# A new table of instruction orders for a fused cluster-attention, Fourier and feed-forward kernel on one Trainium2 core

## The chip, the cores and the metric

The kernel is one program on one core of one Trainium2 chip. Its metric is the device time of an execution in microseconds (us). The core has five instruction streams that run beside each other and meet at semaphores: TensorE (PE in the profile; PEld is its loading of weights into the array), VectorE (DVE), ScalarE (ACT), GpSimd (POOL) and SyncE (SP), which here does nothing but issue DMAs. Each stream runs its instructions strictly in the order in which they stand in the program.

## What is computed

Four sequences of 768 tokens go through clustered attention with 8 heads of 64, then through a two-dimensional Fourier transform with a residual, a normalization and a feed-forward layer of 512 to 2048 to 512:

```python
mask = q_assign[:, :, :, None] == k_assign[:, :, None, :]
scores = scale * np.matmul(q, k.transpose(0, 1, 3, 2))
scores = np.where(mask, scores, -1000000000.0)
attn = np.exp(scores - np.max(scores, axis=-1, keepdims=True))
attn = attn / (np.sum(attn, axis=-1, keepdims=True) + 1e-09)
x = np.matmul(attn, v)
...
mixed = np.real(np.fft.fft(np.fft.fft(x, axis=1), axis=2))
u = x + mixed
un = (u - mu) / np.sqrt(var + 1e-06)
out = u + np.maximum(un @ w_ch1, 0.0) @ w_ch2
```

The cluster of a query or key is the centroid of largest cosine; the mask keeps pairs of the same cluster.

## The kernel before

All matrix products are made of float16 pieces (a high and a low half), so that each product of the reference is three matmuls.

**Attention.** The 32 heads are taken as 16 pairs, and each pair as six blocks of 128 queries. For one block `Attention.scores` writes the scores of both heads into the two buffers `ps_big` of PSUM. In pairs 0 to 7 these are matmuls of line 538, which use 64 rows of the array each, one head in the upper and one in the lower half, and four mask matmuls of 32 rows (line 543); in pairs 8 to 15 they are the matmuls of line 530, over the whole height. For each head DVE then scales and finds the row's extreme (line 557), ACT takes the exponential (line 560) and rounds it (line 568, tile `ph` or `p`), POOL makes the low half (line 569), and SP issues a DMA that transposes the 128x1536 result into `pts` or `u` (line 571). Two blocks later `Attention.attend` multiplies by v (lines 589 to 591, 18 matmuls per head, tile `ps_o`), and `finish` divides (lines 601 to 605).

**Weights.** Meanwhile `Weights` loads both matrices in 32 pieces (line 715, 512 KB each), finds their scales (line 725) and splits them (lines 754, 758, 764 to 770).

**Layer.** When the four pairs of a sequence are done, its layer runs beside the attention of the next sequence: folding (line 899; line 904 is its transposing DMA), tables from HBM (lines 972 to 982), the transform (lines 991 to 1069), the normalization (line 1120 and about), the up product (line 1286, 160 groups of 12 matmuls into PSUM banks `ps_fa`, `ps_fb`, `ps_fc`, drained by lines 1291 to 1295) and the down product (line 1314, drained by line 1318). For the last sequence, lines 1177 and 1228 to 1253 do two thirds of the up product with fewer multiplications.

**The order.** The code records all instructions in one pass. Then `Order.apply` (in the class `Order`) takes a permutation for each engine out of the table `ORDERS`, a compressed list of 16-bit numbers, and chains the engine's instructions in it:

```python
by = np.cumsum(np.frombuffer(zlib.decompress(base64.b85decode(ORDERS[e])), np.int16))
xs = [xs[n] for n in np.argsort(np.arange(len(xs)) + by)]
for a, b in zip(xs, xs[1:]):
    self.tc.add_manual_dep(b, a.name, ...)
```

Tiles, buffers, banks and dependencies were fixed by the recording; the table alone says which instruction of an engine stands behind which.

Of the kernel before, what the change touches and what calls it, by code (L numbers as in the profile page):

```python
# [26 lines left out]
P = 128  # L27
B, H, S, D = 4, 8, 768, 64
# [4 lines left out]
SH = S // 2  # L33
# [34 lines left out]
class Counted:  # L68
# [5 lines left out]
    def tile(self, shape, dt, name, bufs=None, **kw):  # L74
# [6 lines left out]
        "c-m!E*>2Q85G;?!dyx?3P=fM+1W16y|9=Hf@CG6h2qXyNNV4o{dz<R&@d9Ek+vAz(?&|95SpcZ8v&47ed(5w`ZLG6n#INSv8j#W8qxts{_td;w`%"  # L81
        "b%4+1EJ3OY3cdOMZ8DXBF;ql<~oqc8Nod-PSF9bWq~m@;btdD?3`;+Lj(>T<I;-|COEMggz1$*3fIqr@w0?Vd#iw%ekN2eMalfrkqb&aeR$p-Ev&"
        "fYiA=y$?_9<)r<prY^~BtWa4uNd~TJ+NFFoRT=DS;H}tc#8KYjnF*jVBaL1H0&f3a6w;!DE^_^%@GuD`6&uvLYoX<+vXR`L7puVv~+Kk2f9izlA<"
        "E=eWCV{wN&d!fBmhjFV!N<LM)-j8cNxUm;im#;H7IqI=Y;5@T7`~qH-h8KL;`Z)s#~rO^2ZcD6mOIuK-aBD!Z6uptM4x0)?-d2@a&F^y$~t{vl|I"
        "QHitW)Rs#sE_5x=9d(_-bbjjHVkdJBA&qWLr8jEKPTWjO9$N*i*IoO1EDrS-OO5|!^uo-vd4T#CtHsVQ??+ZCLUvTEGZIFXYqep@QTV>`l)`pLU$"
        "Za#MPy7k<GpCP}wg%*H`d`0Y9os>DAs#mh=)JQ3=55OzGV7xc-)|LF4qLj7u(%Aw1hjKg@uU@bPaZpPsEA>YDk8RKRg%D?4m8?3c8M2Q^6`3D85A"
        "r{#HPo1>eedDk2IiU)Y0XI98Eg5Ddqs??sM|65y|FXKKi>CZL<j{Wv9>CB!+Y?#v|w|%=2CZDU8z^-Y$fi7{43?{?Br72r7Dy#>{^z*fN_br)`{c"
        "RQ=Ju!`eJ1daV>piss(s1{nmJ8VO^Cxvg*4kd>-RlQDfG5u-Nk!YVth`#hMfat!=ii*o^3oxc&^UZRoKXqHZ3cm4~N1Ie<7b0(bRSw`D10A+<*pb"
        "2$Y9<3!92=%dQ9uj47Ou+Zz=nmwm=sn>GfKSR7f9)^2s3H3koJ4@xODrZV9&)0TNUhi|X*`Jr*FQNH!uAlHf2W0dIae2?2aCF3z7P!#rjpqCm|7t"
        "_$jKqsqa4Ke3e7EAM(c67{A5DS6Yo}9rEaZKuw=?t`V5Bny"  # L90
    ),
    "Pool": (
        "c-l==?M~EC5S`wBvb(S=f)b2|m>7+T{`N_HMc=@LKfVKM3{goy(I|$9EbLdeJ)SwYD{j*6?R4hM%$YMadtev1WhWTg6!+{iYV>W%(+PI%3|H8;eS"
        "3*xG^lKh+h$gy#R91X%lMS=3cOOg#2I62+_jH*B71y0N1>>KehUQ4t%31sutd*VB#d41K1ZpTq5WZoROc}^80DVE*p~i|nb|dRog9D1eiAF|{BwI"
        "|hj9CpF=bc9jCS{S+)NcERuM6=-^|e9ksZ)u%5E3R<v44KO&Oapresvsbunfa3HvxAM+2Lv183nEE4-u3!3uS@`VINkS?Zbd`+*s9Wp^Gj@v<jAg"
        "N=B<qEBx7^s1QMYskAS&U(SK+ZxVo%4##R=e6~TQg;5K%lnXBoMVmg1yP5r_7JB;TC%@deNDx5kBs_%MXyZr$kkJ#E)sU{_iLWV7!Ym1xJ>NKafB"
        "E44URU(mYHg8G#_Uv)$GljJMYkQx8g4<r&RVSK4Fu-ZhepE;wJVx!3-niY1oIWBr0Z&F>#(7tS08E?5(gf+oXmjoR!D#(JNP7eMS#y+wbz{s>ZeF"
        "GhLU(XA!d(WVn#p=BT8CsPt`4vnKimvp63^+TLiQuJyod1$jRb>I_jaZmXr<1tP13Dwq*DB}T<Jd-fHpxlQq%_$4vj>QnWYRn<W#j_R0!S(A?IR{"
        "32=16HuZ-OlxVL3Rsr;y#%+%{_gi3gX3yw21q>;Dr0+()YocJwOoph|gPg%BKk)Gp0|hK4*8%Ey(N@;yiP89d~n=x^Vtn>y36g))~aZKpPbqb=|+"
        "iQ{t_whSXjo5u?j4a@T$!leSvid~-@EqLFrUodcDTv4S9dx&0dF+>cHAR*b3@9cx&M#n36yQ3@%)rGMQqa*X?Yw_-Nd?{$sz^ab&Ib+hT=-zoX;-"  # L100
        "*-0dcVWJ-Dd%&F)fdmYjq`kQ-#k~zm`l#r>vpB|c)yS~Tk6F%?V5~VzFdrY)L*G**&q"
    ),
# [26 lines left out]
    "PE": (
        "c-rk8ZEO@(@b#`9&|E(#HB{^e!nL+VT50Qns1+$fsfvkT2#tshiJ&B!C`Ljg8bw>RQDcmvrl@HQ+8X&Gi7_C=)L67?m5PRt5UU{=`~dujBH_8aw`"  # L130
        "<?-?d+Smn`_d9N$#%qc6Mgoyf>fwu3=%qDQUikg+GL>_nf5h3hVu#6oC*5zAXA>GUr=_9xg=SJg<?h3K;J&?t548zy?5uLi;n<dVj{i8bDB+iojV"
        "fvjVR_Yw#+_;+fqtjfOYNuqaTz*NSYhE^&oPzwH_cOw9_!Yzq;*mTP!@Xk0(WG_RE!UcJEeA!B?7)9T)%kzu2CJ!ZVjHLkR^*e_$E#k`wI6KxtPE"
        "@j+J*J^mhjn_^KXMl-gtJM3seEaXHrR}*|pDOGX(ZNy~OvzlqHq<P#wHS*v^ZWp~{-U`mOuD{HBSVjM{chvc$;9zyL<EW}-}f5$9ZbCIG`!o*d0I"
# [728 lines left out]
class Fourier:  # L862
# [7 lines left out]
    EF, AM, EM = 20480, 36992, (42208, 43936)  # L870
# [455 lines left out]
class Overlap:  # L1326
# [4 lines left out]
    T0, LAG = 5, 2  # L1331
# [257 lines left out]
```

## Time and profile before

| what | value |
|---|---|
| time, median of 3 executions | 954.57 us |
| lowest and highest | 952.27 and 954.65 us |
| span of the profiled execution, first to last instruction | 949.3 us |
| PE busy | 863.9 us (91%) |
| DVE, ACT, POOL busy | 678.2, 601.6, 608.3 us |
| mean granted TensorE clock | 0.976 of full speed |

Of the profiled execution only the span is listed, not a time of its own; the timed executions lie 3.0 to 5.4 us above that span. An engine's busy time is the union of its instructions, so what is missing to the span is idle time. An idle stretch is put down to what ended it ("DVE ... <- PE ...": DVE waited for PE); "issue" means that the profile shows no wait. DMA share is the mean busy share of the 16 DMA engines and can go over 1 where packets overlap.

### The profile page before, as it was taken

The page shows a single profiled execution, that of the slowest core. Times are in us where ns is not written, and L with a number is a line of the kernel's source. Part 1 is how long each engine was busy: PE and PEld are TensorE (multiplying, and loading weights), DVE is VectorE, ACT ScalarE, POOL GpSimd, SP SyncE. Part 2 cuts the span into 40 slices and gives each one's busy share as a digit, 9 for nine tenths or more (in the row PEclk, how much of TensorE's full clock was granted, in tenths as well). Part 3 has the DMA queues.
Part 4 walks back from the last instruction along what each step waited for, and adds up shares of the span by engine and source line. Part 5 has one row for each costly group of instructions (what it writes and reads, how often), then busy time and mean ns, then how long its engine had stood idle before and what let it go on. Part 6 is the DMA issues. An engine that isn't in the chain of part 4 may idle for free.

```text
span 949.3 us, 23660 instructions
## 1 busy us (share of the span) xinstructions
PE 863.9 (91%) x9241; PEld 581.0 (61%) x9241; DVE 678.2 (71%) x1531; ACT 601.6 (63%) x944; POOL 608.3 (64%) x752
## 2 busy tenths in 40 slices
PE   4777776677999999998999999999999999999998
PEld 1334443345756748666758667667668586676674
DVE  7989888877756667677757567678773446889643
ACT  6989988776666747647757747657676563353320
POOL 3778786755876876746767768748677764342421
PEclk9999897889999999999999999999999999999999
DMA  9999999988588888999899889998887764201020
GB/s 360 242 217 192 233 262 222 224 169 159 103 169 144 146 178 164 184 177 173 157 171 184 174 155 187 197 173 187 151 147 153 132 118 101 60 1 41 19 78 23
DMA packets 405151, 150.20 MB, mean 158 GB/s; under 512 B 383024, under 2 KB 391728, under 8 KB 405040
## 3 DMA queue, kind: packets, MB, share of 16 engines
q1 hardware_dynamic: 404896, 148.67, 78.1%
q8 instruction: 72, 1.18, 0.5%
q14 instruction: 39, 0.32, 0.1%
q10 hardware_dynamic: 144, 0.03, 0.0%
HBM read 41.99 MB, written 6.29 MB: 51 GB/s over the span
## 4 chain that ended last, share of the span: by engine, by line
PE 56%; DMA 7%; DVE 5%; POOL 4%; ACT 4%; issue 2%; SPq 1%; ACTq 0%; POOLq 0%; DVEq 0%
PE ps_fb L1314 8%; PE ps_fc L1314 7%; DMA pts<-ph 7%; PE ps_fa L1286 6%; PE ps_fa L1314 5%; PE ps_fb L1286 5%; PE ps_fc L1286 5%; PE ps_big L530 5%; PE ps_big L1228 3%; POOL ph L569 2%; PE ps_o L589 2%; PE ps_o L590 2%; PE ps_o L591 2%; PE ps_big L538 1%; ACT ph L568 1%
## 5 line engine op out<-in xcount | busy, mean ns | idle before, releaser
L569 POOL TENSOR_TENSOR ph<-p,ph 128x768 f16<-128x768 f32 x144 | 238.4, 1656 | 112.8 <-ACT ph L568 96.8
L557 DVE TENSOR_SCALAR_CACHE_REDUCE ps_big<-ps_big,sce 128x768 f32<-128x768 f32 x144 | 145.4, 1020 | 60.5 <-PE ps_big L530 34.7
L1314 PEld LDWEIGHTS <-arena 128*128 128x128 f16 x1152 | 109.9, 98 | 121.4 <-issue 1.6
L560 ACT ACTIVATE p<-ps_big,rmx 128x768 f32<-128x768 f32 x144 | 128.7, 897 | 60.3 <-DVE ps_big L557 43.0
L568 ACT CAST ph<-p 128x768 f16<-128x768 f32 x144 | 119.6, 830 | 70.0 <-DMA pts<-ph 67.7
L1295 POOL TENSOR_TENSOR arena<-arena 128x256 f16<-128x256 f32 x160 | 110.8, 697 | 52.2 <-ACT arena L1294 51.6
L1286 PEld LDWEIGHTS <-w1h 128*128 128x128 f16 x1280 | 124.9, 98 | 17.9 <-issue 1.5
L589 PE MATMUL ps_o<-v,pts 128*128 128x66 f16 x1062 | 111.1, 194 | 3.9 <-DMA pts<-ph 2.1
L590 PE MATMUL ps_o<-v,pts 128*128 128x64 f16 x1062 | 110.3, 195 | 0.0
L591 PE MATMUL ps_o<-v,pts 128*128 128x66 f16 x1062 | 110.0, 193 | 0.0
L589 PEld LDWEIGHTS <-pts 128*128 128x128 f16 x1062 | 98.4, 97 | 13.7 <-issue 5.9
L590 PEld LDWEIGHTS <-pts 128*128 128x128 f16 x1062 | 98.4, 97 | 7.4 <-issue 2.6
L1314 PE MATMUL ps_fb<-w2h,arena 128*128 128x512 f16 x320 | 100.9, 379 | 0.0
L591 PEld LDWEIGHTS <-pts 128*128 128x128 f16 x1062 | 98.6, 99 | 0.4
L538 PE MATMUL ps_big<-u 64*128 64x384 f16 x576 | 71.7, 356 | 26.2 <-ACT p L560 13.0
L1286 PE MATMUL ps_fa<-arena,w1h 128*128 128x256 f16 x464 | 85.5, 273 | 0.0
L1314 PE MATMUL ps_fc<-w2h,arena 128*128 128x512 f16 x256 | 81.0, 379 | 0.3 <-ACT arena L1294 0.3
L1286 PE MATMUL ps_fb<-arena,w1h 128*128 128x256 f16 x424 | 78.3, 273 | 0.7 <-DVE arena L1056 0.4
L530 PE MATMUL ps_big<-u 96*128 96x384 f16 (+1 forms) x384 | 75.6, 325 | 2.4 <-ACT p L560 2.3
L1286 PE MATMUL ps_fc<-arena,w1h 128*128 128x256 f16 x392 | 72.4, 273 | 1.1 <-ACT arena L1294 1.1
L1286 PEld LDWEIGHTS <-w1l 128*128 128x128 f16 x640 | 62.5, 98 | 10.6 <-issue 1.6
L538 PEld LDWEIGHTS <-u 64*128 64x128 f16 x576 | 30.1, 100 | 54.3 <-issue 33.9
(371 smaller groups left out, 2149.2 us busy)
## 6 DMA issues: line engine op xcount, KB each, us to landing
arena<-in_moe_w_ch_dram SPq DMA_DIRECT2D x26, 512.0 KB, 5.6
scr<-in_k_dram SPq DMA_DIRECT2D x16, 384.0 KB, 4.3
scr<-in_q_dram SPq DMA_DIRECT2D x16, 384.0 KB, 4.2
vst<-in_v_dram SPq DMA_DIRECT2D x16, 384.0 KB, 4.1
out_dram<-arena SPq DMA_DIRECT2D x24, 256.0 KB, 2.8
u<-u SPq DMA_DIRECT2D x64, 96.0 KB, 2.7
u<-u SPq DMA_DIRECT2D x16, 192.0 KB, 3.2
pts<-ph SPq DMA_TRANSPOSE x161, 3.9
```

What stands on the lines that cost most here:

```text
L530: nc.tensor.matmul(out=ps[j][:, hf, 0:SH], lhsT=self.slots(x + 2 * j, 1)[0:n, sl], rhs=self.slots(y + 2 * j, 1)[0:n, hf * SH:(hf + 1) * SH ...
L538: nc.tensor.matmul(out=ps[j][:, hf, 0:SH], lhsT=hq[rows[j], a, sl], rhs=hk[rows[j], c, hs], start=(i == 0), stop=False)
L557: self.mark = nc.vector.tensor_scalar(out=ju, in0=ps[j][:, :, 0:SH], scalar1=ne, scalar2=None, op0=ALU.mult, op1=ALU.min, accum_out=m)
L560: nc.scalar.activation(x, ju, AF.Exp, bias=m, scale=-1.0)
L568: nc.scalar.copy(out=ph[:, 0], in_=p32)
L569: nc.gpsimd.tensor_tensor(out=ph[:, 1], in0=p32, in1=ph[:, 0], op=ALU.subtract)
L589: nc.tensor.matmul(out=o[:, at:at + W], lhsT=hi, rhs=v16[:, kt, 0:W], start=(kt == 0), stop=False)
L590: nc.tensor.matmul(out=o[:, at:at + D], lhsT=hi, rhs=v16[:, kt, 66:130], start=False, stop=False)
L591: nc.tensor.matmul(out=o[:, at:at + W], lhsT=lo, rhs=v16[:, kt, 0:W], start=False, stop=(kt == ST - 1))
L1286: nc.tensor.matmul(out=ps.rearrange("p (t x) -> p t x", x=P), lhsT=a[:, dc, fs], rhs=c[:, :, dc], start=(i == 0), stop=(i == 11))
L1295: nc.gpsimd.tensor_tensor(out=hl[:, f], in0=r, in1=hh[:, f], op=ALU.subtract)
L1314: nc.tensor.matmul(out=ps, lhsT=a[:, f, ts], rhs=w[:, f], start=(i == 0), stop=(i == 47))
```

## The change

The table `ORDERS` is replaced for all five engines. Not a line of the recording changes: the instructions, their tiles and the data that they pass are the same, 18,404 of PE, 1,338 of DVE, 944 of ACT, 748 of POOL and 498 of SP. The new table is longer, so every line number behind it grows by 19 (line 538 becomes 557, 571 becomes 590).

```diff
 ORDERS = {
     "Activation": (
...
     "PE": (
-        "c-rk8ZEO@(@b#`9&|E(#HB{^e!nL+VT50Qns1+$fsfvkT2#tshiJ&B!C`Ljg8bw>RQDcmvrl@HQ+8X&Gi7_C=)L67?m5PRt5UU{=`~dujBH_8aw`"
...
+        "c-qxld8{Nw8LzJHp6Qu4Gw*);-o9mbS#ZH+cUc6C$hF}xauY;M6b;d!YZeg|H4=;`>K`H~F(3v!Ks1CPBpx8Ax&{aumSZ)5h=Rc40?N58;(S(DeO3KccUO"
...
```

Most instructions move, but not far: by 2.5 places on average on ACT, 3.3 on SP, 5 on POOL, 8 on DVE and 30 on PE. Markers stay where they were: the first eviction of the up product (line 1291) is DVE's 387th instruction before and its 390th after, the first of the transform (line 884) its 323rd and 325th.

**First place: PE, the second block of scores, near the start.** `ps_big_324` and `ps_big_325` are the score buffers of the two heads; `ps_fa_650` and `ps_fb_730` are banks in which weights are worked on. Before, on PE:

```order
L543 MATMUL ps_big_287<-u_109 128x384
L754 LDWEIGHTS arena_67
L754 MATMUL ps_fa_650<-arena_67 128x512
L754 LDWEIGHTS arena_67
L754 MATMUL ps_fa_650<-arena_67 128x512
L538 LDWEIGHTS u_109
L538 MATMUL ps_big_324<-u_109 128x384
L538 LDWEIGHTS u_109
L538 MATMUL ps_big_325<-u_109 128x384
```

After (lines 19 higher):

```order
L773 MATMUL ps_fa_650<-arena_67 128x512
L557 LDWEIGHTS u_109
L557 MATMUL ps_big_324<-u_109 128x384
L744 LDWEIGHTS arena_67
L744 MATMUL ps_fb_730<-arena_67 128x512
L744 LDWEIGHTS arena_67
L744 MATMUL ps_fb_730<-arena_67 128x512
L773 LDWEIGHTS arena_67
L773 MATMUL ps_fa_650<-arena_67 128x512
L557 LDWEIGHTS u_109
L557 MATMUL ps_big_325<-u_109 128x384
```

The first matmul of head 0 is parted from the first of head 1: three matmuls of the weights, which use the whole height of the array, now stand between them. Counted over the whole program, the matmuls of line 538 stand in 55 unbroken runs before and in 137 after; of these, 41 and 121 lie in what ran in the first 250 us. The passes over the array that the runs need, where two heads side by side share one, rise from 209 to 239 in that stretch.

**Second place: SP, about the folding of the first sequence.** `ph_2632` to `ph_2772` are rounded exponentials to be transposed; `scr_2791` and `vst_2474` receive q, k and v of later pairs. Before, on SP:

```order
L571 DMA_TRANSPOSE pts_110<-ph_2632 128x12x128
L904 DMA_TRANSPOSE arena_67<-arena_67 128x12x128
L372 DMA scr_2791<-in_q_dram 128x768
L352 DMA vst_2474<-in_v_dram 128x768
L372 DMA scr_2791<-in_k_dram 128x768
L571 DMA_TRANSPOSE pts_110<-ph_2640 128x12x128
L904 DMA_TRANSPOSE arena_67<-arena_67 128x12x128
L571 DMA_TRANSPOSE pts_110<-ph_2764 128x12x128
L972 DMA arena_67<-in_cd_dram 128x516
L980 DMA arena_67<-in_cs_dram 128x6x128
L571 DMA_TRANSPOSE u_109<-ph_2772 128x12x128
```

After:

```order
L391 DMA scr_2791<-in_q_dram 128x768
L391 DMA scr_2791<-in_k_dram 128x768
L590 DMA_TRANSPOSE pts_110<-ph_2554 128x12x128
L991 DMA arena_67<-in_sd_dram 128x516
L590 DMA_TRANSPOSE pts_110<-ph_2632 128x12x128
L923 DMA_TRANSPOSE arena_67<-arena_67 128x12x128 x2
L590 DMA_TRANSPOSE pts_110<-ph_2640 128x12x128
L590 DMA_TRANSPOSE pts_110<-ph_2764 128x12x128
L991 DMA arena_67<-in_cd_dram 128x516
L999 DMA arena_67<-in_cs_dram 128x6x128
L999 DMA arena_67<-in_ss_dram 128x6x128
L590 DMA_TRANSPOSE u_109<-ph_2772 128x12x128
```

The loads of q and k stand earlier, that of v later, and the two transposes of the folding follow each other; ahead of the transpose of `ph_2772` there are now three table loads instead of two. Counted from the first transpose of line 571 to the 54th, 13 transposes stand right behind a plain copy before, and 18 after.

## Rows read from the trace of the kernel before

**Rows 1.** The page's head and its first part: busy us, share of span, instructions.

```profile
span 949.3 us, 23660 instructions
PE 863.9 (91%) x9241; PEld 581.0 (61%) x9241; DVE 678.2 (71%) x1531; ACT 601.6 (63%) x944; POOL 608.3 (64%) x752
```

**Rows 2.** Five stretches: length, busy us of PE, PEld, DVE, ACT, POOL; clock, DMA.

```profile
0.00:25.00 25.00, 10.67 (x62) 4.88 (x63) 19.89 (x53) 16.06 (x22) 7.31 (x52) 1.00 0.92 363
25.00:200.00 175.00, 123.84 (x1532) 66.35 (x1532) 155.49 (x324) 150.90 (x195) 132.22 (x116) 0.89 1.08 226
200.00:250.00 50.00, 43.29 (x575) 32.48 (x573) 37.65 (x100) 34.16 (x58) 32.88 (x40) 0.95 0.76 134
250.00:925.00 675.00, 665.75 (x6937) 465.97 (x6934) 456.12 (x1034) 398.13 (x667) 432.73 (x537) 1.00 0.73 140
925.00:949.30 24.30, 20.40 (x148) 11.27 (x146) 9.06 (x23) 2.37 (x4) 3.15 (x9) 0.99 0.06 22
```

**Rows 3.** Waits of PE and PEld, 25 to 200 us: total us, times, longest.

```profile
PE ps_big L538 <- DVE X L557: 12.9, 17, 1.8
PE ps_big L538 <- ACT p L560: 9.4, 5, 4.2
...
PEld L538 <- DVE X L557: 8.0, 8, 1.9
```

**Rows 4.** Waits of DVE for PE, 25 to 200 us.

```profile
DVE ps_big L557 <- PE ps_big L543: 2.6, 3, 1.9
DVE ps_fb L758 <- PE ps_fb L754: 2.3, 2, 1.8
DVE X L557 <- PE ps_big L543: 2.3, 4, 1.1
...
DVE arena L728 <- PE ps_fa L725: 1.1, 2, 0.9
DVE rs L601 <- PE ps_o L591: 1.1, 1, 1.1
```

**Rows 5.** Waits of DVE for PE, 200 to 250 us.

```profile
DVE ps_big L557 <- PE ps_big L543: 3.6, 4, 1.9
...
DVE arena L1291 <- PE ps_fb L1286: 1.3, 1, 1.3
```

**Rows 6.** Timeline of PE at 303 us: start us, us, engine, line, operation.

```profile
302.99 0.27 PE L1286 MATMUL ps_fa<-arena,w1l 128*128 128x256 f16 x1
303.10 0.27 PE L1286 MATMUL ps_fa<-arena,w1h 128*128 128x256 f16 x1
303.30 1.15 PE L538 MATMUL ps_big<-u 64*128 64x384 f16 x12
304.38 0.34 PE L543 MATMUL ps_big<-u 32*128 32x384 bf16 x4
304.65 0.20 PE L590 MATMUL ps_o<-v,pts 128*128 128x64 f16 x1
```

**Rows 7.** DMA issues, 25 to 200 us: count, median us from issue to landing.

```profile
pts<-ph SPq DMA_TRANSPOSE x29, 4.1
pts<-p SPq DMA_TRANSPOSE x16, 4.5
```

**Rows 8.** The same view, 250 to 780 us.

```profile
pts<-ph SPq DMA_TRANSPOSE x122, 3.9
```

**Rows 9.** The chain that ended last, 200 to 233 us: start us, us, what.

```profile
200.37 5.42 DMA u<-ph
...
232.88 1.31 PE ps_fa L1286 x12
```

**Rows 10.** Waits of ACT and POOL for DMA, 25 to 200 us.

```profile
ACT ph L568 <- DMA pts<-ph: 2.8, 4, 0.8
...
POOL p L566 <- DMA u<-p: 1.7, 2, 0.9
```

**Rows 11.** Costliest groups, 25 to 200 us: count, busy us, mean ns, idle before.

```profile
L557 DVE TENSOR_SCALAR_CACHE_REDUCE X<-ps_big,sce 128x768 f32<-128x768 f32 x48 | 47.9, 1011 | 6.2 <-PE ps_big L543 2.3 <-POOL ph L569 1.8 <-POOL ac L443 1.1
```

More of the change, by code (lines that the diff above doesn't have):

```diff
@@ L85 @@
[L85 to L89, printed above, removed]
@@ new lines @@
+        "%skHLPWboYv17u{PS<%NQ7=R%fhAu_ZCsvYrcYdPr<Jt^usFT?C7kvmUR`XC&W~MMlYF0ndy!QGBLM-)A38T0-9w+nKpq?m^N`)6^9SS&2HmpEi||GvatR"
+        "I!1ouy+N!c;|@4e7V&+m_!Db2+>u@Cag&$o+67{Cvu&tX+D(!$o8_%EvU8a@&Kf(C5&0S$cZuH-vc$cf8=i6(X{smiHNP>o;3c|oH^kR=*7mcT;!)yoPD#"
+        "OCbq)g0g21;(KfBg?j$T`ZhO%UauseAyQ^|86V|Q}#`<y&`$1?8J0A4*ZWUQL6oo=@Ckr53?PWuhewq(@4CH2-@@5?gvC(0n9sI;4QJKMUmW~FA~XlAf@h"
+        "wK%${G-OSPcb33+RDVwYx%1_u{rBq?sd#D_=MQrItrWkiWrT(3D2)wz9pWFPv@lCu{0#MQ*d%3w;IWJw<AUB&McjeLVMqx1!E49?aMZFyA|R6Onx)D1Dj)"
@@ L96 @@
[L96 to L100, printed above, removed]
@@ new lines @@
+        "!tal~tlW&iTF&RisVzXty`0{xKEsX8j?1#L*5bLM1oJTN$^kFm_eh^_ern%6c-u7T$B_9Ph2MACSvjlzSyl$oZ0fH;B5Dg8pxeyR(WXMDaHD%2;z&#y%>b"
+        "JyUfHn_Xv&4vE*Hf6qMjnCBLr5wW0NIycTRy4;n3k!bf~wXH?WB+f)(87d;Fm(KMzep_YgJ(Cfy+qB;2bSt|$)vcU8HH&$?agROHNS8LK7S;7FcR1&B&VA"
+        "iCMY7bhIG@W@b1iWL<36p}&%VuB?ASYrGu-80z)w-ukC0oWyFLY8O6;EQ@Kuk-M9SzDIH^~BwLiK&1@xqdjMuQs8pg6^lfOlc26#oRoGiu?ySAWG16t0A9"
+        "1uIyS`{PP{@kW_VN>YS&U#Zrx8$4cY;O9Oi2gduNIvmYi5#`osYJV{W<66To@a`zoeQ=bfw+y$o1SL*^;!1+FSE`p>3MY~jHpY%xoui&mvYT*(;LgBS1ae"
@@ new lines @@
+        "l|>~o+_99M1et9v>lyIN`?V;$?PBr;Gtx6?dw<)KQD^v_r#{0<?X$RFB~DOT0zlJxXP$QM$o-Fr?x)9UU6JtebP?dk$F*v>_{j??FP^LI!`0hvJiM7z2|b"
+        "hc+Fhrrq7J^Q{P?`wk9-_R<uM2UOQ@r2yeRC2uS={&89TmVi(9pmo+@{Ty1{E4$ejfkcP36V!2VK+|8ec1JQzK~aW=Huo6BG@W*nd>dcugSI^;YLd`M9=Z"
+        "NBz;6PlegrmZZM*EvD?=M?M)%y*VW*S$U|+zmq<EzI-p3+>u9d*;jPphxjBM1vux+<@{KOlQST!QzpA0%!E*=apWw!8h(ZMWXMuIZ9FDa~Tfb=ryfN2Dh;"
+        "$*VwXP%J>q2?~2wHMOJ-$Nj$P(gNVBLe~XF{gT|5m*&p|g<l`1@Rc0;UFbEV?CZIGLe@$!_AgN+#L4WpRR>Ihio#`*?0*zlr-RL9>tpQ?<x#0DUeN#bb?L"
@@ new lines @@
+        "Y7tq>kUvL`me85t?T&i3#nP8I^%_pi;yIiw!$t%~+(srM`eNP-c8BmJ54UW!p_k=5_3U><Z4pgz`y!$nF@GtLS21zakuWxg0bxTvl(!KVM-5}O45!G6aWu"
+        "lpa&FiX=vtS*^p@J4F{`T!Tn$-9l@!!IB$F&A5q0muR?g};qW4aYqtcYcXlv>b2yt7y6ELIHshUTX<P}|$#~2-vIcVMl$1?nGsc|O?Ra>&|wsGb?Y0zesr"
+        "&#W~HS~-YJxgFO4j9ej7#w|1UkRElM<dP1(gQN|6yo_kP}uqw?CfcU&8jzp|Fig=LVJ_`SLi)A5<C;;!dGsG@qE#Z$}6xv)q#4xMB!F}jCrpt{uaTp4iS@"
+        "5eUuK=BolcC9%k^w7_pC9PSFd5_Zq;IkVB8lHFgQ(kZ^AW{bfq;cZkX}%(HzCH+wiWRC6Id_Ds+*_w_pD&xqw_PtATG&vp3{$mhh{u%4HrvcE#~le$72`q"
```

115 lines of the change are left out of this document (64 added, 51 removed).

## The prediction

> **What bounds the kernel now.** I read the busy times first. PE is busy in 863.9 of 949.3 us, far ahead of every other engine [rows 1], so the first question is where its 85.4 idle microseconds lie. The stretches tell it [rows 2]: 14.3 in the first 25 us, 51.2 from 25 to 200, 6.7 from 200 to 250, 9.3 in the 675 us from 250 to 925, and 3.9 at the end. From 250 us on PE is busy 98.6% of the time, and an order can give back 9.3 us there at the very most. Only the first 250 us are loose, and there PE is not the bound: from 25 to 200 us DVE is busy 155.5 of 175 us, ACT 150.9, PE 123.8, while the DMA engines are busy 108% [rows 2]. So the time is made of a start whose pace DVE sets, with ACT and the transfers close behind, and of a long PE-bound remainder whose amount of work no order changes. What a new order can earn is a shorter start (DVE idles 19.5 us from 25 to 200 and 12.4 us from 200 to 250) and a part of those 9.3 us.
>
> Then the waits. PE in the start stands mostly behind a score buffer that is not free: its next instruction is a score matmul, DVE or ACT still reads `ps_big`, and all that is queued behind it on PE waits too. The three rows of this kind make 30.3 us, though the one of the weight loads can be partly the same time as that of the matmuls [rows 3]. In the other direction DVE waited for PE 9.4 us in five rows between 25 and 200 us [rows 4] and 4.9 us in two rows between 200 and 250 [rows 5]. These 14.3 us are what better timing on PE could return on the engine that sets the pace.
>
> **The change, part by part.** No instruction is added or removed, so the busy work is the same and each term is a wait.
>
> *Filled stalls on PE (gain).* The first place in the order shows the pattern: after the first matmul of head 0, which can start when its buffer is free, PE now does three weight matmuls instead of standing until DVE has freed the buffer of head 1. In effect products of weights and of attention come earlier, and with them what DVE waits for. On the path lies only what DVE waited for, 14.3 us [rows 4, 5]; the bounds are 0 (the scores themselves come no sooner, since DVE frees their buffers at the same pace) and 14.3. I take half, 7.2 us, as there is no row that tells how many of these waits were of PE's own making.
>
> *Detours between tile shapes (cost).* A score matmul of line 538 uses 64 rows of the array, a weight or attention matmul all 128. The timeline shows what the change between them costs [rows 6]: one up matmul follows another after 0.11 us (302.99 to 303.10), but the first score matmul comes 0.20 us after the last of them, so 0.09 us are lost on the way in. The twelve score matmuls, six passes, and the change to the 32-row form take 1.08 us, 0.165 a pass if that change costs 0.09 too. Then the change from the 32-row form back to the full height, 0.27 us less such a pass, costs about 0.10. A detour out of the score form and back costs both, 0.19 us. The new order has 121 runs of score matmuls in the first 250 us instead of 41, so 80 more detours: 15.2 us of PE time. It also needs 239 passes instead of 209, since heads that were side by side are parted: 30 x 0.16 = 4.8 us more. The sum is 20.0 us of PE. Cover: PE idles 51.2 us from 25 to 200 [rows 2], and the detours stand where it would have waited anyway. If that cover is gone, scores come later and DVE, which does line 557 next, waits. Bounds: 0 and 20.0 us. From 25 to 200 us DVE waited for PE in 9.4 of 175 us, so I let 5% of most of it count, 0.9 us; from 200 to 250, where PE is busy 43.3 of 50 us, seven of the detours count in full, 1.3 us. Together 2.2 us.
>
> *Transposes behind copies (cost).* 18 transposes instead of 13 stand right behind a copy. A transpose landed in a median of 4.1 or 4.5 us in the crowded start [rows 7], in 3.9 us later [rows 8], and the one that lay on the chain near 200 us, with table loads about it, in 5.42 us [rows 9]. That puts the price at 0 to 1.5 us each, 7.5 us for the five at most. But only six landings out of 45 were waited for by ACT or POOL, 4.5 us in all [rows 10]. I take 5 x 1.5 x 6/45 = 1.0 us.
>
> *Loads about the first folding.* q and k go earlier and v later, so the two folding transposes are no longer parted by three loads. The chain near 200 us runs through the transpose of `ph_2772`, however, and not through them [rows 9], and that one now has three table loads ahead of it. I cost this at nothing: its cover is that transpose, and its bounds are a gain or a loss of 1.5 us, the difference between 5.42 and 3.9.
>
> *The PE-bound remainder (gain).* Of 9.3 idle us I take 2 us; bounds 0 and 9.3, and a loss has no clear limit there, as PE's three banks can also be drained worse.
>
> *Fetches of instructions.* Each engine has as many instructions as before and no row names a wait for a fetch, so there is no term.
>
> Sum: -7.2 + 2.2 + 1.0 + 0 - 2.0 = -6.0 us on a span of 949.3, that is 943.3. The median of the timed executions is 5.3 us above the span of the profiled one, so the forecast is 954.57 - 6.0 = **948.5 us**. A measurement of this kernel can tell about 0.3%, 2.9 us, from no change: below 951.7 counts as faster, above 957.4 as slower.
>
> **Rivals.**
>
> *Slower: the detours reach DVE.* Place: the score matmuls from 25 to 250 us. For: 20.0 us of PE work is added in the loop that goes from DVE freeing a buffer to PE's scores and back to DVE; if half of it is late for DVE, 10 us come on the path, against a filled-stall gain that shrinks to half as well, 3.6 us. With 1.0 for the transposes and 2.0 back later that is -3.6 + 10.0 + 1.0 - 2.0 = +5.4, so 960. Against: from 25 to 200 us DVE has 155.5 - 47.9 = 107.6 us of other work beside 48 passes of line 557 [rows 2, 11], some 4 us for each block of two passes, and a block's scores take 1.35 us now (303.30 to 304.65) [rows 6]. Spread over the 34 blocks of the first 250 us, 20.0 us make 0.6 us each, and 1.95 is still below 4. It decides where a block's scores come more than some 4 us after their buffer is free; that DVE was waiting for scores seven times in that stretch already [rows 4] shows that such blocks exist. The Trainium skill, TensorEngine Tiling (Array Packing), section Key Properties, says that changing the tiling mode, and not just the tile, drains TensorE; by that rule each detour pays twice. The trace agrees, with the 0.09 and 0.10 us of [rows 6]. Chance 0.22.
>
> *No change.* The moves are short: the markers of transform and up product stand within three places of where they stood on DVE, so DVE has the same work ahead of the PE-bound part. If a filled stall on PE only moves PE's idle time to the end of a block, gain and cost cancel: 954.6. For: PE is not the bound there, and 5 us more or less of costs in the terms above do it. Against: DVE did wait for PE. Chance 0.24.
>
> *Faster by much.* All 14.3 us of DVE's waits for PE and half of the 9.3 us return, less 2.2: -16.8, so 938. For: almost every instruction was placed anew. Against: DVE idles for ACT and POOL as well, and PE's detours are real. Chance 0.08.
>
> **How the numbers follow.** The forecast, a gain of 3 to 14 us, has 0.46; with the large gain, faster has 0.54. No change has 0.24 and slower 0.22. The likeliest case alone spans 941 to 951.7. The range reaches down to the large gain's 938 and up to the slower rival's own 960; beyond it I leave about 0.05 below and 0.10 above.
>
> **What would show it.** Right: DVE's idle time from 25 to 200 us falls below 15 us; PE's waits for `ps_big` in that stretch fall well below 30 us while PE's busy time there rises by 10 us or more from the detours; the first up product, at 232.9 us before [rows 9], starts 4 to 5 us earlier; PE stays above 98% from 250 to 925 us. Wrong on the side of slower: DVE's waits for line 562 (the old 543) grow, and the up product starts later. Wrong in kind: the start is unchanged and the difference lies behind 250 us, where I allow 2 us, or landings of transposes move by more than 1 us at the median.

## The result, and the profile after

| | median us | lowest to highest | executions |
|---|---|---|---|
| before | 952.97 | 950.92 to 956.18 | 7 |
| after | 958.72 | 952.29 to 962.48 | 7 |

The new order is 0.56% slower: ratio 1.0056, with a 95% interval of 1.0028 to 1.0083, some 5 us where 6 us less were forecast. The profiled execution of after took 962.48 us and is the slowest of its seven, so its trace shows somewhat more of the loss than the median does. The page's head and its first part:

```profile
span 960.8 us, 23673 instructions
PE 887.9 (92%) x9241; PEld 589.4 (61%) x9241; DVE 680.5 (71%) x1531; ACT 604.9 (63%) x944; POOL 612.9 (64%) x752
```

PE is busy 24 us more than before [rows 1], with the same instructions. The same stretches as in [rows 2], in the same columns:

```profile
0.00:25.00 25.00, 12.86 (x54) 5.16 (x56) 18.35 (x52) 15.01 (x20) 7.18 (x50) 0.96 0.87 348
25.00:200.00 175.00, 145.56 (x1609) 76.19 (x1606) 152.14 (x333) 155.59 (x204) 139.50 (x126) 0.89 1.11 231
200.00:250.00 50.00, 45.98 (x595) 34.48 (x592) 42.84 (x99) 34.74 (x60) 31.76 (x41) 1.00 0.74 137
250.00:925.00 675.00, 651.72 (x6690) 452.92 (x6688) 452.21 (x1011) 393.23 (x652) 426.62 (x516) 0.99 0.73 139
925.00:960.80 35.80, 31.78 (x303) 20.62 (x301) 14.98 (x41) 6.33 (x12) 7.84 (x20) 1.00 0.04 16
```

Two things stand in them. In the first 250 us PE idles 12.1 + 29.4 + 4.0 = 45.6 us instead of 72.2. From 250 to 925 us it idles 23.3 us instead of 9.3: the part that I had called a long PE-bound remainder is where the time went. The start did come out ahead. One line's instructions, the up product, with first and last start:

```profile
L1305 PE MATMUL ps_fb<-arena,w1h x424: 270/273/283, 226.2 to 854.5; 128*128 128x256 f16 x142
```

It begins at 226.2 us, 6.7 us earlier than the 232.9 of [rows 9]. Followed by equal amounts of finished PE work through both traces (each matmul counted with the time after which its like follow one another), after is 6.9 us ahead at 240 us and still 6.3 at 320; it then loses in steps, is level at 517 us, 5.0 behind at 600, 8.0 at 650 and 11.6 at 770, and stays there to the end (steps good to about 1 us). So 6.9 us were won and 18.5 lost, the loss between 340 and 770 us. PE's waits from 250 to 925 us name what is new there (total us, times, longest):

```profile
PE ps_big L549 <- DMA u<-u: 8.8, 6, 2.2
PE ps_big L549 <- ACT p L579: 5.5, 5, 1.9
PE ps_fa L1010 <- DMA arena<-in_cs_dram: 2.5, 2, 1.8
PE ps_fa L1010 <- ACT arena L1074: 1.8, 1, 1.8
```

Line 549 (530 before) is the score matmul of pairs 8 to 15. The transfers `u<-u` that it waits for are the 14 copies which `Attention.place` (lines 510 to 517 before, 529 to 536 after) issues on SP for each of these pairs: pieces of q, k and masks, moved to other rows and slots of the tile `u`, so that two products fit into one matmul of the whole height. All pairs share the same slots. So the copies of a pair wait for the last scores of the pair before it, and its first scores wait for the copies. Before, no wait for `u<-u` stood in this view. One of the six, in the timeline of PE at pair 9 (in brackets the idle time ahead and what ended it):

```profile
417.20 0.19 PE L609 MATMUL ps_o<-v,pts 128*128 128x64 f16 x1
419.27 0.48 PE L549 MATMUL ps_big<-u 128*128 128x384 f16 x2 [1.89 <-DMA u<-u]
419.60 0.27 PE L1010 MATMUL ps_fa<-arena 128*128 128x258 f16 x1
```

The matmuls of line 1010 behind it were ready; in a strict order they had to wait too. SP in the same microseconds (start, time that the issue took):

```profile
417.48 2.45 SPq L590 DMA_TRANSPOSE pts<-ph  x1
419.98 0.59 SPq L531 DMA_DIRECT2D u<-u  x1
420.61 0.60 SPq L532 DMA_DIRECT2D u<-u  x1
421.25 0.59 SPq L536 DMA_DIRECT2D u<-u  x1
421.95 0.54 SPq L533 DMA_DIRECT2D u<-u  x1
422.59 1.48 SPq L590 DMA_TRANSPOSE pts<-ph  x1
424.12 0.89 SPq L529 DMA_DIRECT2D u<-u  x1
425.07 1.27 SPq L536 DMA_DIRECT2D u<-u  x1
426.44 1.43 SPq L590 DMA_TRANSPOSE pts<-ph  x1
```

In these 10 us SP issues one DMA behind the other without a pause, copies and transposes mixed. It did so about pair 9 before as well; what changed is the time at which PE comes for the copies. Before, PE began the first score of pair 9 at 424.8 us, and the last copy that landed ahead of it did so at 423.8. After, PE was there at 417.4, 7.4 us earlier, while the copies stood hardly earlier (the first issued at 407.1 instead of 408.5 us): the copy that PE waited for was issued at 416.1 and landed at 419.0. Between the last score matmul of one pair and the first of the next, counted in the two orders, PE now has less to do in sum:

```diff
 matmuls between the scores of pairs 8|9, 9|10, 10|11, 11|12, 12|13, 13|14, 14|15
-58  96  117   69  115   86  162
+56  22   91  111   75   37  146
```

That is 538 matmuls instead of 703. Pair by pair, however, the count doesn't go with the stalls: pairs 9 and 12 waited, with 56 for 58 and 111 for 69 matmuls ahead of them, and the first block of pair 10 didn't, with 22 for 96. The places of the copies on SP moved too.

Two of the six stalls cost more than their own length. PE stood 2.18 us until 585.17, and then the granted clock fell, in part of the next 5 us, to the lower of its two levels, from 2.4 to 1.2 GHz (columns as in [rows 2]):

```profile
580.00:585.00 5.00, 2.98 (x28) 2.52 (x26) 0.13 (x1) 2.91 (x7) 2.94 (x4) 1.00 0.69 133
585.00:590.00 5.00, 4.83 (x45) 3.50 (x45) 2.92 (x7) 3.31 (x6) 3.15 (x4) 0.66 0.84 161
```

The same follows the stall that ends at 643.62 us, where PE had stood 1.75 and then 1.02 us. An estimate from these rows is (1 - 0.66) x 5 = 1.7 us of TensorE work for each, 3.4 of the 18.5 us lost in this trace. Before, the clock was 1.00 all through these 675 us [rows 2].

### The profile page after: what moved, and what is told of

The parts are those of the page before. It is cut to its first block, busy times and chain, and to the rows that moved or that the text cites. A ratio compares the mean times of both kernels' runs of the same rounds, so it can differ in the third digit from the quotient of the medians.

```text
span 960.8 us, 23673 instructions
## 1 busy us (share of the span) xinstructions
PE 887.9 (92%) x9241; PEld 589.4 (61%) x9241; DVE 680.5 (71%) x1531; ACT 604.9 (63%) x944; POOL 612.9 (64%) x752
## 4 chain that ended last, share of the span: by engine, by line
PE 52%; DMA 16%; ACT 9%; POOL 8%; DVE 8%; issue 5%; SPq 2%; POOLq 0%; ACTq 0%; DVEq 0%
DMA pts<-ph 10%; PE ps_fb L1333 6%; PE ps_fc L1333 6%; PE ps_fa L1305 5%; PE ps_fa L1333 5%; POOL ph L588 5%; PE ps_fb L1305 4%; PE ps_fc L1305 4%; PE ps_big L549 4%; ACT ph L587 3%; PE ps_big L1247 3%; PE ps_big L557 2%; PE ps_o L609 2%; PE ps_o L610 2%; PE ps_o L608 2%
## 5 line engine op out<-in xcount | busy, mean ns | idle before, releaser
L1333 PEld LDWEIGHTS <-arena 128*128 128x128 f16 x1152 | 102.2, 97 | 85.0 <-issue 3.2
L608 PE MATMUL ps_o<-v,pts 128*128 128x66 f16 x1062 | 144.3, 197 | 4.7 <-DMA pts<-ph 3.2
L610 PE MATMUL ps_o<-v,pts 128*128 128x66 f16 x1062 | 142.9, 196 | 0.0
L609 PE MATMUL ps_o<-v,pts 128*128 128x64 f16 x1062 | 142.7, 197 | 0.0
L610 PEld LDWEIGHTS <-pts 128*128 128x128 f16 x1062 | 102.1, 100 | 28.7 <-issue 14.8
L608 PEld LDWEIGHTS <-pts 128*128 128x128 f16 x1062 | 102.1, 99 | 28.6 <-issue 7.0
L609 PEld LDWEIGHTS <-pts 128*128 128x128 f16 x1062 | 101.7, 99 | 28.7 <-issue 14.9
L1333 PE MATMUL ps_fb<-w2h,arena 128*128 128x512 f16 x320 | 111.3, 379 | 0.0
L549 PE MATMUL ps_big<-u 128*128 128x384 f16 (+1 forms) x384 | 88.1, 327 | 14.3 <-DMA u<-u 8.8
L557 PE MATMUL ps_big<-u 64*128 64x384 f16 x576 | 82.8, 346 | 17.3 <-DVE X L576 11.1
L1305 PE MATMUL ps_fa<-arena,w1h 128*128 128x256 f16 x464 | 92.5, 275 | 0.3 <-ACT arena L1313 0.3
L1333 PE MATMUL ps_fc<-w2h,arena 128*128 128x512 f16 x256 | 89.5, 379 | 0.0
L1333 PE MATMUL ps_fa<-w2h,arena 128*128 128x512 f16 x192 | 65.8, 379 | 0.5 <-DVE arena L1076 0.3
```

Source lines behind the costliest of these rows:

```text
L549: nc.tensor.matmul(out=ps[j][:, hf, 0:SH], lhsT=self.slots(x + 2 * j, 1)[0:n, sl], rhs=self.slots(y + 2 * j, 1)[0:n, hf * SH:(hf + 1) * SH ...
L557: nc.tensor.matmul(out=ps[j][:, hf, 0:SH], lhsT=hq[rows[j], a, sl], rhs=hk[rows[j], c, hs], start=(i == 0), stop=False)
L608: nc.tensor.matmul(out=o[:, at:at + W], lhsT=hi, rhs=v16[:, kt, 0:W], start=(kt == 0), stop=False)
L609: nc.tensor.matmul(out=o[:, at:at + D], lhsT=hi, rhs=v16[:, kt, 66:130], start=False, stop=False)
L610: nc.tensor.matmul(out=o[:, at:at + W], lhsT=lo, rhs=v16[:, kt, 0:W], start=False, stop=(kt == ST - 1))
L1305: nc.tensor.matmul(out=ps.rearrange("p (t x) -> p t x", x=P), lhsT=a[:, dc, fs], rhs=c[:, :, dc], start=(i == 0), stop=(i == 11))
```

## The experiments

Ratios are to the kernel before, timed on the same chip in the same batch; 0.1% is about 1 us.

**Which part of the order loses.** The kernel with the new start follows the new order in everything that began in the first 242 us before, and the old order behind; the one with the new rest is its counterpart.

```diff
 instructions that started before 242 us | all others
-old order                               | old order
+new order                               | old order      (new start)
+old order                               | new order      (new rest)
```

> Each engine follows the new order in what ran in the first 242 us before, and the old order in all behind that. My theory, from the two traces: the new order gains about 7 us in the start and loses it, and more, between 350 and 780 us. Then this kernel keeps the gain: 5 to 8 us faster than before (ratio 0.992 to 0.995). Rival, the detours between tile shapes make the new order slow, in the start as well: no gain, ratio 1.000 to 1.006. Rival, the gain at 242 us is only PE work moved ahead that the old remainder cannot use: ratio 0.997 to 1.001.

> The counterpart: the old order in what ran in the first 242 us before, the new one in all behind it. My theory: slower than before by 8 to 18 us (ratio 1.008 to 1.019), with PE waiting at the score matmuls of line 530 for the copies of q and k into the upper rows, as in the profile after. Rival, the loss arises only because the new start hands over to the rest earlier than the loads and transposes can follow: within 3 us of before (0.997 to 1.003).

New start: 950.77 us, ratio 0.9981 (0.9964 to 0.9999). New rest: 963.67 us, ratio 1.0114 (1.0095 to 1.0133), with these waits of PE from 250 to 925 us:

```profile
PE ps_big L547 <- DMA u<-u: 6.8, 5, 2.5
PE ps_big L547 <- ACT p L577: 5.3, 5, 2.3
PE ps_fa L1008 <- DMA arena<-in_cs_dram: 2.6, 2, 2.3
```

The loss is in the rest and doesn't need the new start: in this trace PE comes for the first score of pair 9 at 422.1 us, 2.7 earlier than before, and the copies of that pair begin at 412.0, 3.5 later. The start is a gain, but a small one: 1.8 us of the 6.9 that it was ahead. Its profiled execution (948.33 us, 2.4 below its median) lost 1.6 us where it goes over to the old order. The parts, -1.8 and +10.9, make +9.1; the whole change is +5.3 (2.7 to 7.9), so they don't simply add.

A later cut, ahead of the first copies, was to keep the whole of the gain:

```diff
-started before 242 us
+started before 335 us
```

> The new order in what ran in the first 335 us before, which ends ahead of the first of these copies (345 us), the old order behind. If the new order loses at the copies alone, this keeps all of its gain without the early handover at 242 us (where the kernel with the new start lost 1.6 us of 6.7): 4 to 7 us faster than before, ratio 0.993 to 0.996. Rival, the handover costs the same wherever it lies: ratio 0.997 to 1.000, as with the new start alone (0.9981).

955.03 us, ratio 1.0031 (1.0014 to 1.0049): a miss on both sides. In its trace PE idles 3.6 us between 250 and 345 us, against 0.1 in the new start's. Why the handover costs more there than at 242 us was not found.

**Detours, and one engine alone.** In the next kernel the start is the new one, but each block's score matmuls stand together again, so that line 538 forms 48 unbroken runs instead of 135.

```diff
 PE, first 242 us, one block
-L538 (head 0) | L725, L754 ... | L538 (head 1) | ...
+L725, L754 ... | L538 (head 0, head 1), L543 | ...
```

> The new order in the start as in the kernel with the new start alone, but with the 64-row score matmuls and the mask matmuls of each block put together again, at the place of the block's last one, so that the detours are gone. My term says that nearly all of the detours' 20 us of PE time is hidden: within 2.2 us of the kernel with the new start alone. Rival, detours reach DVE: 4 us or more faster than that one. Third possibility, parting the heads is what fills PE's stalls: 4 us or more slower than that one, PE's waits for ps_big back at about 20 to 30 us between 25 and 200 us.

953.93 us, ratio 1.0023 (1.0001 to 1.0045), by the ratios 4 us slower than with the detours (0.9981), with some 1 to 7 us as the interval of that difference. The stretch from 25 to 200 us, first of the new start, then of the gathered kernel:

```profile
25.00:200.00 175.00, 144.62 (x1605) 74.13 (x1601) 152.28 (x332) 155.35 (x203) 138.49 (x126) 0.89 1.09 229
```

```profile
25.00:200.00 175.00, 123.73 (x1585) 69.25 (x1582) 150.88 (x329) 152.61 (x199) 137.14 (x125) 0.90 1.06 228
```

Gathering takes 20.9 us of PE time away, and all of it comes back as idle time. But the sign that the third possibility named did not come: PE's waits for DVE and ACT at `ps_big` fell further, from 13.0 to 7.8 us. What grew is DVE's wait for the scores, 7.7 us in the new start:

```profile
DVE X L559 <- PE ps_big L545: 13.8, 10, 3.4
```

Gathered at the place of the block's last one, the scores of head 0 come later, DVE waits for them, and the up product begins at 229.0 us instead of 226.7. The clock differs too: over the timed executions its mean is 0.973 here, as in the kernel before, and 0.979 in the new start. How much of the 4 us each of the two makes was not separated.

The kernel with SP alone in the new order of the start:

```diff
 first 242 us
-PE, DVE, ACT, POOL old | SP old
+PE, DVE, ACT, POOL old | SP new
```

> The old order on all engines but SP, whose DMAs of the first 242 us stand in the new order. If the start's gain comes from PE's filled stalls, as I put it, SP alone gives nothing: within 1.5 us of before (0.9985 to 1.0015), or a loss of about 1 us by the transposes behind copies. Rival, the moved loads and transposes make the gain: 3 to 7 us faster.

984.37 us, ratio 1.0344 (1.0321 to 1.0367). Neither reading foresaw 32 us. SP's waits from 25 to 250 us:

```profile
SPq L715 <- DVE ps_fb L758: 15.4, 5, 9.8
SPq L571 <- POOL p L569: 13.9, 9, 3.1
SPq L571 <- POOL arena L935: 11.2, 1, 11.2
```

A transfer whose source isn't ready, or whose target isn't free, on the other engines' old schedule holds all behind it, once for 11.2 us. The orders of the engines fit each other and can't be judged one at a time.

**Are PE's stalls the price?** First I took the stalls out: the score matmuls of line 530 that stood waiting were placed later by their stall and 0.5 us more, with what depends on them; for copies only, then for copies and ACT, then the latter in the changed kernel itself.

```diff
 PE, pair 9 (the other stalled blocks alike)
-... | first scores | 2.5 us of L1008, L606 to L608 | ...
+... | 2.5 us of L1008, L606 to L608 | first scores | ...
```

> Base: the kernel with the old start and the new rest (963.67 us, ratio 1.0114). In its trace PE stood 6.8 us in five stalls at the first scores of a pair, for the copies of q and k into the upper rows. Here these score matmuls, in pairs 8, 9, 12 and 13, stand later in PE's order by the length of their stall and 0.5 us more, behind PE work that is ready (and what follows from them on the other engines goes with them); SP is untouched. If a stall of PE in this stretch costs the time one for one: 5 to 7 us faster than the base, ratio 1.004 to 1.006 against before. Rival, the copies are late because of SP and the stall only moves to the next score: within 2 us of the base, ratio 1.010 to 1.013.

> As in the kernel with the first scores later, and the four score matmuls of line 530 too that stood 5.0 us for ACT, which still read the score buffer (pairs 9, 11, 14 and 15). One for one: 11 to 12 us faster than the base with the new rest (963.67), so that nothing is left of the loss, ratio 0.998 to 1.001 against before. Rival, these stalls are idle time that would come up elsewhere, since ACT sets the pace of the scores: no faster than the kernel that moves the first scores alone.

> The changed kernel itself (958.72 us, ratio 1.0056), with the score matmuls of line 530 that stalled in its trace for copies or for ACT (14.1 us in nine blocks of pairs 8, 9, 10, 11, 12, 13, 14 and 15) placed later by their stall and 0.5 us. If the stalls are the whole of its loss: 10 to 14 us faster than the changed kernel, 945 to 949 us, ratio 0.991 to 0.996 against before, which would beat both kernels. Rival, something else in the new rest holds it (drains, table loads, the transposes): ratio above 1.001.

All three got slower: 968.32 us, ratio 1.0193 (1.0166 to 1.0219); 972.33, 1.0220 (1.0193 to 1.0246); 964.42, 1.0141 (1.0115 to 1.0166). In the first the waits for copies fell from 6.8 to 0.5 us, and others took their place:

```profile
PE ps_big L548 <- ACT p L578: 10.7, 10, 2.6
PE ps_fa L1304 <- ACT arena L1312: 2.6, 3, 1.7
PE ps_fa L1009 <- ACT arena L1073: 2.6, 1, 2.6
```

Scores that come later hold ACT at the exponential: its wait there for DVE, which takes the scores first, rose from 14.0 us in the new rest to 20.6 (345 to 765 us). PE then waits longer for what ACT frees behind that: for the score buffers 10.7 us instead of 5.3, for the banks of the other products 7.6 instead of 2.9. My theory that PE's order is merely too early fell here. (The trace is that of the slowest of six executions, 974.41 us.)

Then I moved the same scores in the kernel before, where no such stall was: 4 us earlier, and 4 us later.

```diff
 PE, kernel before: matmuls between the scores of pairs 8|9 ... 14|15
-58   96  117   69  115   86  162
+35   72   68   18   65   68  124    (earlier)
+105 131  144  111  153  149  184    (later)
```

> The kernel before, with one thing changed: the first block's score matmuls of each of the pairs 8 to 15 stand 4 us of PE work earlier in PE's order (3.5 us in pair 8); the copies stay where SP had them. Before, these matmuls started 0.3 to 3 us after the moment at which they would have had to wait for a copy, by the landings in its trace, so 4 us too early makes stalls of 2.0, 3.6, 3.7, 1.2, 2.7, 3.1, 1.7 and 1.7 us, 19.7 in sum. One for one: 15 to 20 us slower than before, ratio 1.016 to 1.021, PE's waits for the copies at 15 us or more. Rival, PE catches up because the work it was ahead of is done later in time that was idle: within 4 us of before.

> The kernel before with the first block's score matmuls of pairs 8 to 15 placed 4 us later in PE's order (and what follows from them on the other engines). The counterpart of the kernel that had them 4 us earlier and lost 19.7 us. If only stalls for copies count, later is harmless: within 2 us of before. If the scores are tied from both sides, because ACT's exponential stands ahead of the drains that PE's products wait for, as the kernels with later scores in the new rest suggest: 5 to 15 us slower (ratio 1.005 to 1.016), with PE waiting for ACT at ps_fa, ps_fb and ps_fc.

Earlier: 969.72 us, ratio 1.0208 (1.0181 to 1.0234), so 19.7 us for 19.7 forecast. Later: 968.73 us, ratio 1.0167 (1.0142 to 1.0192), 16.4 us and more than the 5 to 15 forecast. PE's waits in them from 250 to 925 us, first of the earlier, then of the later:

```profile
PE ps_big L531 <- DMA u<-u: 14.7, 10, 3.1
PE ps_big L531 <- ACT p L561: 3.9, 5, 1.7
```

```profile
PE ps_big L532 <- ACT p L562: 9.7, 15, 1.4
PE ps_fb L993 <- DVE arena L1320: 2.5, 1, 2.5
```

That the first comes out at exactly 19.7 is in part luck: the waits for copies are 14.7 us, not 19.7, and a clock of 0.992 in these 675 us, with 1.00 before, makes up some 5 us (an estimate, 0.008 x 675). In the second, PE waits for ACT at the score buffer (2.3 us before) and hardly more than before at the banks, where it was foretold. ACT's wait at the exponential, 345 to 765 us, before and in the later kernel:

```profile
ACT p L560 <- DVE ps_big L557: 24.4, 16, 4.0
```

```profile
ACT p L562 <- DVE ps_big L559: 33.9, 21, 5.1
```

So the scores of pairs 8 to 15 are tied from both sides: earlier, PE waits for the copies; later, ACT waits for the scores and PE for ACT. Moving these scores on PE, by 4 us or by the length of the stalls and 0.5 us, cured nothing in any of the five kernels.

**Without the copies.** Here the 112 copies are left out.

```diff
         for j in range(2):
-            nc.sync.dma_start(out=both, in_=q[r, 0:1].broadcast_to([D, 2, S]))
-            nc.sync.dma_start(out=q1[D:P], in_=q[r, 1])
...
```

> The kernel before without the 112 copies of q, k and the masks into the upper rows (the scores of pairs 8 to 15 read what lies there, so only their time counts). In its trace the copies made PE wait nowhere, and no first score started less than 0.3 us after its copies. Theory that the new rest loses by coming too close to these copies: here they cost little, ratio 0.990 to 1.000 against before. Rival, SP as such is short in both orders: 10 us or more faster, ratio below 0.990.

> The kernel with the old start and the new rest (ratio 1.0114), likewise without the 112 copies. If the copies are what the new rest runs into, the loss is gone with them: within 3 us of the kernel before without the copies, and 10 us or more faster than the same kernel with them. Rival, the loss lies in the pace of ACT and of the drains behind it: still 8 us or more slower than the kernel before without the copies, PE's waits for ACT at the scores at 5 us and more.

> The changed kernel (ratio 1.0056), likewise without the copies. By the first theory the gain of the new start shows: 2 to 6 us faster than the kernel before without the copies. By the rival: still slower than that by 3 us or more.

Before: 950.04 us, ratio 0.9974 (0.9959 to 0.9988). New rest: 942.96, 0.9904 (0.9880 to 0.9928). Changed kernel: 939.87, 0.9873 (0.9851 to 0.9895). The copies cost the old order 0.26% and the new one 1.83%, and without them the new order is the faster one by 10.2 us, where 2 to 6 were expected. Most of that is the new rest, not the start: with the old start it is already 7.1 us faster than the old rest, where I had expected 3 at most. The remainder of the changed kernel without copies is what I had thought every order's to be, PE at 99.4%:

```profile
250.00:925.00 675.00, 670.66 (x6975) 469.61 (x6972) 462.26 (x1044) 401.06 (x666) 433.21 (x534) 1.00 0.66 123
```

**In which way they cost.** Three attempts: copies issued but not read, so that no score waits for a copy and no copy for a score; the mask copies alone left out; and the same bytes in 80 DMAs instead of 112.

```diff
-nc.tensor.matmul(out=ps[j][:, hf, 0:SH], lhsT=self.slots(x + 2 * j, 1)[0:n, sl], ...
+nc.tensor.matmul(out=ps[j][:, hf, 0:SH], lhsT=self.other[0:n, 0, sl], ...           (not read)
...
-            for side, x in enumerate((q2, k2)):
-                i = D * side + 32 * j
-                nc.sync.dma_start(out=x[D:D + 32], ...)                             (no masks)
...
-            nc.sync.dma_start(out=k1[0:D], in_=k[r, 1])
-            nc.sync.dma_start(out=k2[0:D], in_=k[r, 0])
+            nc.sync.dma_start(out=self.slots(9 + 2 * j, 2)[0:D]..., in_=k[r])        (merged)
```

> The kernel before with all copies issued as they were, but the scores of pairs 8 to 15 read a constant (pieces of the first weights) in their place, so that no score waits for a copy and no copy for the scores of the pair before it; the scores are thus not the reference's. If the tie between copies and scores is what costs: about the kernel before without copies, ratio 0.995 to 0.999. If the copies' time on SP costs: ratio 0.999 to 1.001.

> The same in the changed kernel: copies issued, scores reading the constant. The changed kernel without copies took 939.87 us, with them 958.72. If it is the tie (last scores of a pair, then 14 copies, then the first scores of the next) that costs the 18.9 us: 939 to 944 us. If it is the time and the places that the copies take on SP, so that transposes and loads behind them are late: 953 to 959 us. In between, each has its share in proportion.

> The changed kernel without the 32 copies of the masks (line 536; 4 of each pair's 14; the scores read what lies there). These are the last in each pair's chain of copies, and the ones that depend on the transposed masks. If the loss goes with the length of the chain between last and first scores: 4/14 of 18.9 us and somewhat more, 951 to 954 us. If it goes with the last copy, whichever it is: below 948 us. If SP's backlog of other DMAs sets the end of the chain: 955 to 959 us.

> The changed kernel with the same bytes copied by 80 DMAs instead of 112: of each head's seven copies, that of q's low half and that of k's high half into the lower rows become one, and those of k's two halves into the upper rows too (k's two slots change roles for it); the merged copy stands in SP's order where the later of the two stood. If the copies' time and places on SP are the main cost (they were 14.6 of 18.9 us by the kernel whose scores don't read them), taking out 32 DMAs should give about what leaving out the 32 mask copies gave, 12.5 us: 945 to 951 us, faster than both kernels. If it is the moment of the last copy, or the bytes: 955 to 959 us.

> The same merging in the kernel before, as the control. There all 112 copies together cost 2.3 us, so this gives 0 to 2 us: ratio 0.998 to 1.000. If it gains as much as in the changed kernel (ratio below 0.993), the merging is good by itself and says nothing of the new order.

| kernel | median us | ratio to before (95%) |
|---|---|---|
| before, copies not read | 952.68 | 1.0018 (1.0001 to 1.0036) |
| changed, copies not read | 954.41 | 1.0021 (1.0000 to 1.0043) |
| changed, no mask copies | 946.21 | 0.9948 (0.9928 to 0.9969) |
| changed, merged copies | 954.69 | 1.0017 (0.9996 to 1.0037) |
| before, merged copies | 950.11 | 0.9990 (0.9971 to 1.0008) |

(Why the kernel before is 0.18% slower when its copies are not read, was not found.) The shares that follow are differences of two ratios, each uncertain by 0.3 to 0.35%. With the tie gone the changed kernel gains 0.35% of the 1.83%. Copies that no score waits for still cost 1.48%, some 14 us. By elimination most of the price is what they do to the other transfers on SP; in which way was not shown. It is not SP's time as such: added up from the traces, SP's issues take 309 of the 420 us from 345 to 765 before and 311 after, 74% in either order, and 57% in the changed kernel without copies. Two effects can be seen. PE's waits for a table load (`in_cs_dram`, 250 to 925 us) are 2.5 us after, 4.2 with the copies not read, 0.4 without the masks and none without copies. And the waits of ACT from 345 to 765 us for the transposes, which have to land before their source `ph` can be written again, move with the copies. Before; after; after without copies; without mask copies; not read; merged:

```profile
ACT ph L568 <- DMA pts<-ph: 60.1, 45, 3.8
```

```profile
ACT ph L587 <- DMA pts<-ph: 78.5, 48, 4.7
```

```profile
ACT ph L580 <- DMA pts<-ph: 37.5, 35, 2.7
```

```profile
ACT ph L586 <- DMA pts<-ph: 60.5, 44, 4.2
```

```profile
ACT ph L587 <- DMA pts<-ph: 74.7, 53, 4.9
```

```profile
ACT ph L588 <- DMA pts<-ph: 62.2, 45, 4.0
```

The row moves with the time, but not in proportion: merged and without masks are nearly equal in it and 8 us apart. In the old order, taking the copies out shortens the same wait too, to 43.5 us, and the time hardly changes; there it lies beside other work. Thirty-two DMAs fewer, with the same bytes, are worth 0.39%: 954.69 us, a miss, since I had expected 945 to 951 if the number of copies is the main cost, and 955 to 959 if it is the moment of the last copy, or the bytes. The mask copies are worth 1.08%, far more than their 32/112, and fall where I had put the moment of the last copy (below 948). Yet when no score waits for the last copy, most of the price stays. The masks are the end of the chain, wait for one transpose more and are bytes besides; which of these it is, stays open, and so does which engine's part of the new order brings the copies and the rest out of step.

A version that beats both came out by the way: the new start with the old rest. It is 0.75% below the changed kernel and 0.19% below the kernel before, less than I had called measurable, though its interval ends below 1.

## Why the prediction was wrong

The forecast was 948.5 us with 0.54 for faster; it is slower, near the 960 of the slower rival, and by another mechanism than that rival's.

- **What bounds the kernel.** The reading "a long PE-bound remainder whose amount of work no order changes" was the error from which the loss followed. A PE at 98.6% [rows 2] showed that the old order covered everything there, not that nothing else was near. I looked for no second limit behind 250 us: neither at the copies, which left no wait in the trace because they were just in time, nor at SP's order. The Trainium skill, Perfetto Trace Analysis, section What "DMA-bound" means, lists as a limit by itself that the issuing engine's sequencer is solid with DMAs. The trace agrees for the 10 us of SP's timeline above, not for the stretch, where SP's issues take 74% in both orders. Moving the scores by four microseconds to either side cost 16 to 20 us.
- **The PE-bound remainder (gain 2 us).** This is the step that failed. I had written that a loss has no clear limit there, but named the draining of the three banks as its way and gave it no price. Instead of a gain of 2 us the new rest alone is a loss of 1.14%, 10.9 us, and the copies carry it: without them the sign turns, and the new rest is 7.1 us faster than the old one. The wait that was missing in the sum is that of PE at the scores of pairs 8 to 15, for copies (8.8 us, none before) and for ACT (5.5 us, 2.3 before), and what the copies do to the transfers behind them.
- **Filled stalls on PE (gain 7.2 us).** The waits for `ps_big` fell as foretold, the two rows of [rows 3] from 12.9 and 9.4 us to

```profile
PE ps_big L557 <- DVE X L576: 11.1, 18, 1.2
...
PE ps_big L557 <- ACT p L579: 2.7, 4, 1.0
```

and PE's busy time from 25 to 200 us rose by 21.7 us. But I priced the term by DVE's waits for PE, and they didn't shrink. From 25 to 200 us the largest, 7.8 us, stands against a largest of 2.6 in [rows 4]:

```profile
DVE X L576 <- PE ps_big L562: 7.8, 9, 2.1
```

DVE's idle time in that stretch grew from 19.5 to 22.9 us instead of falling below 15. What the start gains is PE's own: 26.6 us less idle in the first 250 us, some 20 of them spent on detours, which leaves the 6.6 us by which the up product began earlier. A part of this lead may be the clock, 1.00 instead of 0.95 from 200 to 250 us: at most 2.5 us, an estimate from 0.05 x 50. DVE sets the start's pace, but what a start hands to a PE-bound rest is PE work already done. Of that lead only 1.8 us (0.1 to 3.4) arrived with the old rest behind it, against the 4.0 us of my three terms of the start.
- **Detours between tile shapes (cost 2.2 us).** 20.0 us of PE time were worked out from [rows 6], and gathering took 20.9 us away. That the tiling mode's change drains TensorE, as the Trainium skill says in TensorEngine Tiling (Array Packing), Key Properties, agrees with it. On the path the sign was wrong: the kernel without detours is 4 us slower. There DVE waits longer for the scores of head 0, which parting lets through early; a lower clock may have its share.
- **The slower rival.** Its price, +5.4 us, is close to the measured 5.3, by coincidence: its place was the score matmuls up to 250 us, and they were ahead.
- **Transposes behind copies (cost 1.0 us), loads about the folding (nothing).** Not told apart: SP's part of the start alone, with the other engines' old orders, costs 32 us, which says only that it isn't a part by itself. Two of the six landings in that term, those of `u<-p`, were not among the 45 that it was divided by.
- **What would show it.** The sign named for "wrong in kind", a difference behind 250 us, is what came, with the addition that the start did not stay unchanged.

## What to carry to other kernels

An engine at 98% may be covered by an order that is exact to a few microseconds; before a new order is priced, list for that stretch each transfer that lands just before it is used, and set the moment at which its user comes in the new order against the transfer's place on its own queue; the amount of work ahead of the user alone did not tell which pair would stall. Where two in-order engines are tied by a shared buffer, moving the waiting instruction alone may only move the stall: look at what is queued behind its successor. And take the suspected transfers out altogether, in both kernels: that told in one batch what the moved orders had not.

## What the runs showed of the hardware

- A copy right behind a transposing DMA held SP for 0.87 us at the median (51 of them, 250 to 790 us, both traces), one between two other copies 0.60 us (104 of them); the rows at 424.12 and 420.61 us above are of these kinds.
- From 250 to 925 us the granted clock was 1.00 before and 0.99 after. Behind a stall of PE of 2.2 us, and behind one of 1.0 us that followed another of 1.8, it fell to the lower level for part of the next microseconds (0.66 from 585 to 590 us); behind the other four stalls for copies it did not.
- The spread of a kernel's own executions is wider than the effect of some parts: 948.67 to 960.38 us for the gathered start (12 executions) and 952.29 to 962.48 for the changed kernel (7), against 949.33 to 954.56 for the kernel before (23 in the first batch). One profile can lie 2 to 6 us off its kernel's median, so the steps read from two traces were weighed by timed runs.
